# RWKV-7 recurrence with a squared-ReLU feed-forward: a tile of their own for the small inverse blocks, an earlier transpose, and two weight transfers that change queues

## The chip, the cores and the metric

The kernel runs on one core of a Trainium2 chip. The metric is device time in microseconds, from launch to the end of the last instruction; the time of a kernel is the median of its runs. The profile is that of one execution.

The engines go by these names: PE is the matmul engine (PEld its loading of weights), DVE the vector engine, ACT the scalar engine, POOL the GpSimd engine, SP the engine that here only issues transfers. [...]

## The reference

The first half is a recurrence over 768 tokens for 4 batches of 8 heads with 40 channels each. The second is a feed-forward layer on the 3072 token rows of 320 channels.

```python
B, H, S, D = 4, 8, 768, 40
state = zeros((B, H, D, D))
for t in range(S):
    y[:, :, t] = einsum('bhd,bhde->bhe', rt, state)
    Sa = einsum('bhde,bhe->bhd', state, at)
    state_decay = state * wt[:, :, None, :] - einsum('bhd,bhe->bhde', Sa, bt)
    state = state_decay + einsum('bhd,bhe->bhde', vt, kt)
# y (B, H, S, D) -> x (B*S, H*D) = (3072, 320)
h = maximum(x @ w_in, 0.0)          # w_in (320, 2048)
out = (h * h) @ w_out               # w_out (2048, 320)
```

The weights reach the kernel as 64-bit floats and are turned into 32-bit ones on the chip.

## The kernel before

The kernel cuts the 768 tokens into chunks of 128, so that there are 6 chunks of each of 4 batches, 24 in all. The step from token to token inside a chunk becomes a triangular system per head. Its inverse is solved on POOL (`solve`) and goes through memory (`kept_t`) to the place where the matmuls read it (`inverses`). For the first six chunks (those with `u < FINE`) only the inverses of 32x32 blocks are solved, and PE joins two of them into one of 64x64. Chunk 0 is handled ahead of the main loop, chunks 1 to 5 within it.

These are the parts that the change touches. First, where the short-lived tiles of the joining lie: in slices of `hidden`, the big tile which later holds the hidden layer, or for chunk 5 in the two tiles `own_`.

```python
hidden = single("hid", [128, NF + 1, GB * C])           # NF = 16, GB * C = 256
free_words = hidden.rearrange("p f t -> p (f t)")
wide = [room[:, 4 * WI * i:4 * WI * (i + 1)] for i in range(2)] + [free_words[:, :4 * WI]]
lent = [free_words[:, 2 * DM * i:2 * DM * (i + 1)] for i in range(3)]
own_ = [single(f"raw{i}", [128, 2 * DM]) for i in range(2)]

def spare(name, i):
    n = ("mv", "turned", "blocks", "joins").index(name)
    t_ = hidden[:, NF - 2 * n - i % 2] if i <= B else own_[n // 2][:, n % 2 * H * Q:(n % 2 + 1) * H * Q]
    return t_.rearrange("p (h t) -> p h t", h=H)
```

`wide` and `lent` are the places into which the raw 64-bit weights are fetched: some in the space of the finished weights (`room`, a view of `w_out`), some in the low slices of `hidden`. The raw weights are unpacked piece by piece, some steps per turn of the main loop:

```python
def rounding():
    now = None
    for n in range(len(pieces) + 1):
        before, now = now, None
        if before:
            bits = before[-1]
            nc.scalar.activation(bits, bits, Act.Relu, bias=lowest, scale=float(1 << 23))            # L257
        if n < len(pieces):
            dst, raw = pieces[n]
            words = raw.rearrange("p (f e) -> p f e", e=2)
            nc.scalar.activation(dst, words[:, :, 0].bitcast(U32), Act.Copy, scale=2.0 ** -32)       # L261
        yield
        if before:
            d_, hi, mant, bits = before
            nc.vector.scalar_tensor_tensor(d_.bitcast(I32), hi, -(1 << 31), bits, ...)               # L265
            nc.vector.scalar_tensor_tensor(d_, mant, 2.0 ** -20, d_, Alu.mult, Alu.mult)             # L266
            finished[0] += 1
            for m_ in then.get(n - 1, ()):
                later(lambda m_=m_: fetch_weights(m_, nc.sync), 1)                                   # L248
        if n < len(pieces):
            hi = words[:, :, 1].bitcast(I32)
            # ... two tensor_scalar (L274, L275) and one tensor_tensor (L276) into PSUM ...
            now = dst, hi, mant, bits
        yield
```

Then the joining itself. `queue` is the sync queue.

```python
def inverses(i, g, queue=nc.sync):
    # ...
    if u >= FINE:
        # ... T is loaded from kept_t as it is (L449)
    else:
        blocks = spare("blocks", i)
        for col in range(classes(u)):
            queue.dma_start(out=blocks[col::classes(u)], in_=kept[col].rearrange(...))               # L455
    if "N" not in g:
        # ... loads N from kept_n (L458) and, for the first six chunks, g["joins"] from kept_m (L462)
    if u >= FINE:
        return
    yield
    upper_ = spare("turned", i)
    nc.vector.transpose(upper_.rearrange("p h t -> p (h t)"), blocks.rearrange("p h t -> p (h t)"))  # L467
    for n in range(2):
        nc.scalar.activation(T[:, :, n * Q:(n + 1) * Q], blocks, Act.Copy, scale=which[:, n:n + 1])  # L469
    # ... 16 products of joins and upper_ into p_ (the first small product), p_ to mv (L478)
    yield
    # ... 16 products of mv and blocks (the second small product), to T (L485)
    yield
```

`rest(i + 1)` prepares the next chunk while `chain(i)` runs the present one. The yields are its stages; the main loop takes one stage of each generator in turn, so that they set the order of instructions in each engine's queue.

```python
def rest(i, g):
    # ... stage 2: k transposed
    # stage 3: kvT, ends; joining = inverses(i, g) and, for the early chunks, its first stage (the loads)
    yield
    g["A"] = masked("A", 4, kT, aT)                       # L331
    yield
    # ... rT and vT: r and v transposed by PE, copied by ACT (L513, L515)
    yield
    if c > 0:
        # ... the state times its decay
    g["RV"] = masked("RV", 4, vT, rT)                     # L331
    yield
    # ... the decay transposed by PE (L530)
    yield
    # ... k and b times the inverse decay (L534); the state transposed (L540)
    yield
    yield from joining
    yield
```

`early(m)` works further ahead: it turns the decay of a later chunk and makes its system, with the scans L354 and L355, the reciprocals L358 and L359, bT (L362), aT (L363) and N (L370). `chain(i)` makes xr, minus_x, xnT, RX (L331) and the output tokens (L612). Ahead of the main loop the first weights are fetched beside the solves:

```python
solve(1, {8: lambda: weights_by(0, nc.gpsimd), 20: lambda: take(2, own)})
run(r0)
run(join)
weights_by(2, nc.sync)
solve(2, {4: lambda: weights_by(1, nc.gpsimd)})
```

Fetch 0 feeds pieces 0 and 1 of the unpacking, fetch 1 pieces 2 and 3 (both in the space of `w_out`), fetch 2 pieces 4 and 5 (in the low eight slices of `hidden`). Turn 0 of the main loop unpacks 4 pieces, turn 1 seven, turns 2 and 3 eight each. The first four turns carry no feed-forward matmuls; these begin with turn 4.

Of the kernel before, what the change touches and what calls it, by code (L numbers as in the profile page):

```python
# [17 lines left out]
def kernel(  # L18
# [22 lines left out]
    nc = tc.nc  # L41
    ctx.enter_context(tc.manual_schedule())
    B, H, S, D = r.shape
# [17 lines left out]
    for h, d, n in ((6, 0, D), (7, 0, D), (5, HALF, D - HALF)):  # L61
        while n:
# [5 lines left out]
            d, n = d + m_, n - m_  # L68
# [13 lines left out]
    def psum(pool):  # L82
        name = "ps_" + pool.name[-1]
        return pool.tile([128, 512], FP32, tag=name, name=name)
# [7 lines left out]
    def new(name, shape, bufs):  # L92
        return work.tile(shape, FP32, tag=name, name=name, bufs=bufs)
# [22 lines left out]
    class Ring:  # L116
# [6 lines left out]
        def next(self):  # L123
            self.at = (self.at + 1) % len(self.tiles)
            return self.tiles[self.at]
# [168 lines left out]
    Q = HC // 2  # L294
# [5 lines left out]
    FINE = 4  # L300
# [3 lines left out]
    unit_of = {first + n: u for u, (first, nb) in enumerate(units) for n in range(nb)}  # L304
# [13 lines left out]
    def products(l_, r_):  # L318

        ps = [quads(psum(ps_w)) for _ in range(2)]  # L320
        for q in range(NP):
            for e in range(2):
                rows = slice(e * DP, e * DP + D)
                mm(ps[e][:, q], l_[rows, q, :], r_[rows, q, :], True)
        return ps

    def masked(name, bufs, l_, r_):
        res = []
        for p_ in products(l_, r_):
            t_ = new(name, [128, NP, 128], bufs)  # L330
            nc.vector.tensor_tensor(t_, p_, over4(upper), Alu.mult)  # L331
            res.append(t_)
        return res

    turned = lambda nm, bufs: new(nm, [128, NP, 128], bufs)
# [1 line left out]


    def spare(name, i):
        n = ("mv", "turned", "blocks", "joins").index(name)  # L340
        t_ = hidden[:, NF - 2 * n - i % 2] if i <= B else own_[n // 2][:, n % 2 * H * Q:(n % 2 + 1) * H * Q]
        return t_.rearrange("p (h t) -> p h t", h=H)

# [68 lines left out]
    def solve(u, between={}):  # L412

        first, nb = units[u]
        fine = u < FINE
        size = Q if fine else HC
        cols = classes(u)
        rows = 128 // cols
        part = part_of(u)
        words = size // cols * size  # L420
        at = u * Q * Q // 2 if fine else 0
        ts = solved[:, at:at + words]
        nc.gpsimd.memset(ts, 0.0)
        for col in range(cols):
            nc.gpsimd.memset(ts[col * rows:(col + 1) * rows, col::size + cols], -1.0)
        t3 = ts.rearrange("p (j t) -> p j t", t=size)
        for s in range(size - 1):
            if s in between:
                between[s]()
            n, m_ = s // cols + 1, size - 1 - s  # L430
            at = s * size + s + 1 if s < Q else Q * HC + (s - Q) * (Q + 1) + 1
            p_ = new("half_p", [128, 528], 1)[:, :n * m_].rearrange("p (j t) -> p j t", j=n)
            nc.gpsimd.tensor_tensor(p_, part[:, at:at + m_].unsqueeze(1).to_broadcast([128, n, m_]),  # L433
                                    t3[:, :n, s:s + 1].to_broadcast([128, n, m_]), Alu.mult)
            nc.gpsimd.tensor_tensor(t3[:, :n, s + 1:], t3[:, :n, s + 1:], p_, Alu.subtract)  # L435
        to = kept_t[u]
        to = to.rearrange("n b h f k j t -> (n b h f k) (j t)") if fine else to.rearrange("n b h f j t -> (n b h f) (j t)")
        nc.gpsimd.dma_start(out=to, in_=ts)
# [3 lines left out]
    def inverses(i, g, queue=nc.sync):  # L442
        bb, c = order[i]
        u = unit_of[i]
        kept = kept_t[u][:, i - units[u][0]]
        g["T"] = T = new("T", [128, H, HC], 2)
        if u >= FINE:
            for col in range(classes(u)):
                queue.dma_start(out=T[col::classes(u)], in_=kept[col].rearrange("h f j t -> (f j) h t"))  # L449
        else:  # L450


            blocks = spare("blocks", i)
            for col in range(classes(u)):
                queue.dma_start(out=blocks[col::classes(u)], in_=kept[col].rearrange("h f k j t -> (f k j) h t"))  # L455
        if "N" not in g:
            g["N"] = new("N21", [HC, H, HC], 2)
            queue.dma_start(out=g["N"], in_=kept_n[i])  # L458
            if u < FINE:
                g["joins"] = spare("joins", i)  # L460
                for half in range(2):
                    queue.dma_start(out=g["joins"][half * HC:half * HC + Q], in_=kept_m[i][half])  # L462
# [4 lines that stand above are left out]
        nc.vector.transpose(upper_.rearrange("p h t -> p (h t)"), blocks.rearrange("p h t -> p (h t)"))  # L467
        for n in range(2):
            nc.scalar.activation(T[:, :, n * Q:(n + 1) * Q], blocks, Act.Copy, scale=which[:, n:n + 1])  # L469
        small = lambda: psum(ps_w)[:, :H * Q].rearrange("p (h t) -> p h t", h=H)  # L470
        p_ = small()
        mv = spare("mv", i)
        ends_ = [(slice(half * HC, half * HC + Q), slice(half * HC + Q, (half + 1) * HC)) for half in range(2)]
        for one, two in ends_:
            for h in range(H):
                mm(p_[two, h], g["joins"][one, h], upper_[one, h], True)
        for one, two in ends_:
            nc.scalar.copy(mv[two], p_[two])  # L478
        yield
        p_ = small()  # L480
        for one, two in ends_:
            for h in range(H):
                mm(p_[one, h], mv[two, h], blocks[two, h], True)
        for one, two in ends_:
            nc.scalar.copy(T[one, :, Q:], p_[one])  # L485
        yield
# [4 lines left out]
    def rest(i, g):  # L491
        bb, c = order[i]
        x_ = loaded.pop(i)
        dec = g["dec"]
        up, down, aT = dec[:, UP], dec[:, DOWN], dec[:, A_, :, :C]
        ends = new("ends", [128, NP], 2)
        g["up"], g["aT"] = up, aT
        yield

        kT, rT = turned("kvT", 1), turned("rT", 2)  # L500
        kT_ = turn(x_["k"])
        yield
        nc.vector.tensor_tensor(kT, kT_, down[:, :, 1:C + 1], Alu.mult)
        nc.vector.tensor_copy(ends, down[:, :, 0])
        joining = inverses(i, g) if i else iter(())
        if soon(i):
            next(joining, None)
# [3 lines that stand above are left out]
        while "v" not in x_:  # L511
            line.pop(0)[1]()
        nc.scalar.copy(rT, turn(x_["r"]))  # L513
        vT = turned("kvT", 1)
        nc.scalar.copy(vT, turn(x_["v"]))  # L515
        g["rT"] = rT
        yield
        if c > 0:
            st = states.tiles[bb]
            f_ = new("f", [128, NP, 2], 1)  # L520
            nc.vector.tensor_tensor(f_[:, :, 0], ended[bb], ends, Alu.mult)
            nc.vector.tensor_copy(f_[:, :, 1], f_[:, :, 0])
            nc.vector.tensor_tensor(f_, f_, same, Alu.mult)
            nc.vector.tensor_tensor(st[:, :, :, :D], st[:, :, :, :D],
                                    f_.unsqueeze(3).to_broadcast([128, NP, 2, D]), Alu.mult)
        g["RV"] = masked("RV", 4, vT, rT)
        yield
        p_ = psum(ps_w)
        for q in range(NP):
            nc.tensor.transpose(p_[:, q * 128:(q + 1) * 128], down[:, q, 1:C + 1], ident)  # L530
        inv = p_.rearrange("t (h d) -> t h d", h=H)[:, :, :D]
        yield
        for nm in ("k", "b"):
            nc.vector.tensor_tensor(x_[nm][:, :, :D], inv, x_[nm][:, :, :D], Alu.mult)  # L534
            g[nm] = x_[nm]
        g["v"] = x_["v"]
        if c > 0:
            p_ = psum(ps_c)
            for q in range(NP):
                nc.tensor.transpose(p_[:, q * 128:(q + 1) * 128], st[:, q].rearrange("p e d -> p (e d)"), ident)  # L540
            sd = g["sd"] = new("sd", [128, NP, 2, DP], 2)
            nc.scalar.copy(sd.rearrange("p q e d -> p q (e d)"), quads(p_))
# [3 lines that stand above are left out]
# [159 lines left out]
    def weights_by(n, queue):  # L705
        if weights:
            fetch_weights(n, queue)
# [37 lines left out]
    solve(1, {8: lambda: weights_by(0, nc.gpsimd), 20: lambda: take(2, own)})  # L745
    run(r0)
    run(join)
    weights_by(2, nc.sync)
    solve(2, {4: lambda: weights_by(1, nc.gpsimd)})
    for gen in (e0, e1, e2, e3):  # L750
        run(gen)
    flush()
# [10 lines left out]
    for i in range(len(order)):  # L763
        bb, c = order[i]
        n, before = share.get(i, (TOTAL, 0))
# [56 lines left out]
```

## Time and profile before

| what | value |
|---|---|
| time, median of 3 runs | 1173.26 us (1169.07 to 1174.62) |
| span of the profiled execution | 1171.8 us |
| PE busy | 1041.4 us, 89% of the span |
| POOL busy | 650.8 us, 56% |
| DVE busy | 482.4 us, 41% |
| ACT busy | 245.6 us, 21% |
| moved by DMA | 113.48 MB in 262366 packets, 244164 of them under 512 B |

A line of the page's second part cuts the span into 40 equal slices of 29.3 us; each digit is the busy share of one slice in tenths, and in the line PEclk the share of its full clock that PE was granted. In a timeline, a line gives start and duration, the engine, the source line, the operation and "output<-inputs". A bracket at the end tells how long the engine sat idle before it and what it then had to wait for. SPq is the queue of the sync engine, so its lines are transfers being issued. A line such as L87 or L331 belongs to a helper which many parts of the kernel call; the tile names tell which part it is.

### The profile page before, as it was taken

The numbers are of one execution on the slowest core, as the hardware profiler recorded it, in microseconds if no ns is written. First come the engines' busy times: TensorE is split into PE (matmuls) and PEld (weight loads), VectorE is DVE, ScalarE is ACT, GpSimd is POOL, SyncE is SP. The second block draws the span as 40 slices with busy tenths as digits, with TensorE's granted clock in tenths as the row PEclk, the third lists the DMA queues.
The fourth block names the chain that finished last, engine by engine and source line by source line (L and its number), as shares of the span: only waits on it lengthen the run. The fifth ranks groups of instructions, "written<-read, shape, count | busy, mean of one in ns | idle before, by whom it ended". The sixth has DMA issues, their size and how long they took to land.

```text
span 1171.8 us, 19330 instructions
## 1 busy us (share of the span) xinstructions
PE 1041.4 (89%) x7632; PEld 822.7 (70%) x7632; DVE 482.4 (41%) x1004; ACT 245.6 (21%) x547; POOL 650.8 (56%) x1128
## 2 busy tenths in 40 slices
PE   6496475768999999899899999999999999999998
PEld 5385464655877777777677777777777787777666
DVE  5467474672636515515515514524423243230211
ACT  2123121222222211212211212112122122121211
POOL 5885715882884499950499950599958840000000
PEclk9755555557999998999999999998999999999999
DMA  9989828347454850561861561831444224140000
GB/s 115 158 146 212 164 82 149 116 89 166 77 117 104 163 117 34 105 152 39 155 130 46 96 137 57 169 81 52 95 113 84 56 57 89 24 83 12 6 12 12
DMA packets 262366, 113.48 MB, mean 97 GB/s; under 512 B 244164, under 2 KB 250436, under 8 KB 260612
## 3 DMA queue, kind: packets, MB, share of 16 engines
q1 hardware_dynamic: 257956, 93.24, 39.1%
q0 software_dynamic: 3232, 18.88, 6.6%
q8 instruction: 60, 0.98, 0.4%
q10 hardware_dynamic: 1088, 0.13, 0.1%
q14 instruction: 30, 0.25, 0.1%
HBM read 75.77 MB, written 34.48 MB: 94 GB/s over the span
## 4 chain that ended last, share of the span: by engine, by line
PE 68%; DVE 10%; DMA 9%; SPq 4%; issue 4%; POOL 3%; ACT 2%; DVEq 0%; POOLq 0%; ACTq 0%
PE ps_f L87 32%; PE ps_c L87 19%; PE ps_w L87 11%; DMA in_v<-in_v_dram 4%; PE ps_w L315 4%; SPq L108 2%; DVE decay L358 1%; DMA w_out<-in_moe_w_in_dram 1%; DVE decay L359 1%; PE ps_w L530 1%; POOL half_t L435 1%; POOL half_p L433 1%; PE ps_c L540 1%; SPq L142 1%; SPq L248 1%
## 5 line engine op out<-in xcount | busy, mean ns | idle before, releaser
L433 POOL TENSOR_TENSOR half_p<-half_n,half_t 128x70 f32<-128x70 f32 (+52 forms) x502 | 289.1, 576 | 107.3 <-DMA half_n<-kept_d 57.8
L435 POOL TENSOR_TENSOR half_t<-half_t,half_p 128x70 f32<-128x70 f32 (+52 forms) x502 | 314.3, 626 | 39.3
L640 DVE TENSOR_TENSOR hid<-ps_f,hid 128x256 f32<-128x256 f32 x176 | 73.9, 420 | 343.2 <-ACT hid L639 342.9
L87 PE MATMUL ps_f<-w_out,hid 128*128 128x320 f32 x704 | 207.7, 443 | 0.1
L87 PE MATMUL ps_f<-tokens,w_in 128*128 128x256 f32 x704 | 196.7, 406 | 0.0
L87 PEld LDWEIGHTS ps_f<-w_out,hid 128*128 128x128 f32 x704 | 130.2, 193 | 49.3 <-issue 2.0
L87 PEld LDWEIGHTS ps_f<-tokens,w_in 128*128 128x128 f32 x704 | 123.1, 193 | 42.4 <-issue 29.7
L639 ACT ACTIVATE hid<-ps_f 128x256 f32<-128x256 f32 x176 | 67.4, 383 | 264.3 <-PE ps_f L87 263.9
L87 PE MATMUL ps_f<-tokens,w_third 64*128 64x256 f32 x352 | 85.7, 419 | 6.7 <-DVE hid L640 5.1
L410 POOL DMA_DIRECT2D half_n<-kept_d x18 | 8.9, 502 | 138.5 <-DMA kept_d<-N 138.4
L87 PEld LDWEIGHTS ps_c<-xr,T 64*64 64x64 f32 x768 | 54.4, 149 | 22.0 <-issue 11.7
L87 PE MATMUL ps_c<-xr,T 64*64 64x40 f32 x768 | 60.1, 240 | 5.6 <-DMA T<-kept_t 2.7
L87 PEld LDWEIGHTS ps_f<-tokens,w_third 64*128 64x128 f32 x352 | 39.8, 187 | 33.9 <-DVE hid L640 23.0
L354 DVE TENSOR_TENSOR_SCAN decay<-ps_w,ones 128x64 f32<-128x64 f32 x88 | 23.5, 267 | 85.2 <-PE ps_w L315 77.7
L87 PEld LDWEIGHTS ps_c<-in_v,A 128*128 128x128 f32 x384 | 52.9, 215 | 2.3
L87 PE MATMUL ps_w<-rT,xnT 40*128 40x128 f32 x384 | 37.5, 317 | 16.7 <-DVE RV L331 16.1
L87 PE MATMUL ps_c<-in_v,A 128*128 128x40 f32 x384 | 51.9, 300 | 0.0
L87 PE MATMUL ps_w<-hid 32*32 32x32 f32 x320 | 17.1, 237 | 38.8 <-DVE hid L467 23.8
L87 PEld LDWEIGHTS ps_w<-rT,xnT 40*128 40x128 f32 x384 | 30.9, 214 | 27.0 <-DVE RV L331 22.8
L87 PEld LDWEIGHTS ps_w<-hid 32*32 32x32 f32 x320 | 15.9, 150 | 41.2 <-issue 40.6
L612 DVE TENSOR_TENSOR tokens<-ps_c,dec 128x512 f32<-128x512 f32 x24 | 16.5, 689 | 68.0 <-PE ps_c L87 68.0
L315 PE MATMUL ps_w<-ident,in_ab 128*128 128x128 f32 x192 | 32.1, 318 | 13.8 <-ACT rT L513 9.9
(144 smaller groups left out, 1466.2 us busy)
## 6 DMA issues: line engine op xcount, KB each, us to landing
kept_e<-decay SPq DMA_DIRECT2D x22, 780.0 KB
dec<-kept_e SPq DMA_DIRECT2D x22, 780.0 KB
half_n<-kept_d POOLq DMA_DIRECT2D x12, 384.0 KB, 9.9
half_n<-kept_d POOLq DMA_DIRECT2D x6, 768.0 KB, 11.2
in_w<-in_w_dram SPq DMA_DIRECT2D x24, 160.0 KB
in_ab<-in_b_dram SPq DMA_DIRECT2D x24, 160.0 KB
in_ab<-in_a_dram SPq DMA_DIRECT2D x24, 160.0 KB
in_k<-in_k_dram SPq DMA_DIRECT2D x24, 160.0 KB
```

The costliest lines, as they stand in the source:

```text
L87: nc.tensor.matmul(o, l_, r_, start=start, stop=True, skip_group_check=True)
L108: later(lambda: queue.dma_start(out=out_, in_=in_), steps)
L142: nc.sync.dma_start(out=t_[:, :, :D], in_=src[bb, :, c * C:(c + 1) * C, :].rearrange("h t d -> t h d"))
L248: queue.dma_start(out=to, in_=src.bitcast(I32))
L315: nc.tensor.transpose(p_[:, q * 128:(q + 1) * 128], pair(x_, q), ident)
L354: nc.vector.tensor_tensor_scan(up[:, q, MID + 1:C + 1], wT[:, q, MID:], ones, 1.0, Alu.mult, Alu.mult)
L358: nc.vector.reciprocal(down[:, :, MID + 1:C + 1], up[:, :, MID + 1:C + 1])
L433: nc.gpsimd.tensor_tensor(p_, part[:, at:at + m_].unsqueeze(1).to_broadcast([128, n, m_]), t3[:, :n, s:s + 1].to_broadcast([128, n, m_]), ...
L435: nc.gpsimd.tensor_tensor(t3[:, :n, s + 1:], t3[:, :n, s + 1:], p_, Alu.subtract)
L612: nc.vector.tensor_tensor(t_, y_, g["up"][:, :, :C], Alu.mult)
L639: nc.scalar.activation(h_, p_, Act.Relu)
L640: nc.vector.tensor_tensor(h_, p_, h_, Alu.mult)
```

## The change

The blocks get a tile of their own, one buffer of 128 partitions by 1 KB, instead of a slice of `hidden` (of `own_` for chunk 5). The tiles for the joins move up into the place that this leaves in `spare`. The transposing of the blocks, with their two scaled copies into T, becomes a stage by itself. For chunks 1 to 5 it is taken directly behind the masked product RV, two stages of `rest` sooner than before; the two small products stay where they were. For chunk 0 it stays in place too. Last, weight fetch 1 goes to the sync queue ahead of the third solve and fetch 2 to the GpSimd queue inside it; before it was the other way round.

Its purpose is that the transpose and the copies should be done before PE comes to the first small product, that the blocks no longer share a tile with other data, and that the fetch which is unpacked first is also fetched first.

```diff
-        n = ("mv", "turned", "blocks", "joins").index(name)
+        n = ("mv", "turned", "joins").index(name)
...
-            blocks = spare("blocks", i)
+            blocks = new("blocks", [128, H, Q], 1)
...
         for n in range(2):
             nc.scalar.activation(T[:, :, n * Q:(n + 1) * Q], blocks, Act.Copy, scale=which[:, n:n + 1])
+        yield
         small = lambda: psum(ps_w)[:, :H * Q].rearrange("p (h t) -> p h t", h=H)
...
         g["RV"] = masked("RV", 4, vT, rT)
+        if i and unit_of[i] < FINE:
+            next(joining)
         yield
...
-    weights_by(2, nc.sync)
-    solve(2, {4: lambda: weights_by(1, nc.gpsimd)})
+    weights_by(1, nc.sync)
+    solve(2, {4: lambda: weights_by(2, nc.gpsimd)})
```

## The prediction

> **What bounds the kernel now.** I read the page's slices first, because a share of busy time over the whole span hides that this kernel has two regimes.
>
> ```profile
> PE 1041.4 (89%) x7632; PEld 822.7 (70%) x7632; DVE 482.4 (41%) x1004; ACT 245.6 (21%) x547; POOL 650.8 (56%) x1128
> ...
> PE   6496475768999999899899999999999999999998
> ...
> PEclk9755555557999998999999999998999999999999
> DMA  9989828347454850561861561831444224140000
> ```
>
> One slice is 29.3 us. From the eleventh slice on (about 290 us) PE is busy nine tenths or more at nearly full clock: there the end is set by matmul work, which the change leaves as it is. In the first ten slices PE is half busy at half clock, so something else holds it. All gain or loss must come from there. Next I asked for busy time by stage. The stages are the first turns of the main loop; I took their ends from the timeline (turn 0 starts near 58 us, turn 4, the first that carries feed-forward matmuls, at about 275). Columns: stage, length, busy us of PE, PEld, DVE, ACT and POOL (instructions), granted clock, DMA share, GB/s.
>
> ```profile
> 58.00:107.00 49.00, 35.48 (x312) 32.60 (x310) 31.46 (x59) 13.95 (x27) 39.16 (x115) 0.60 0.85 168
> 107.00:168.00 61.00, 36.65 (x289) 32.94 (x288) 36.68 (x67) 13.53 (x26) 24.65 (x68) 0.50 0.63 138
> 168.00:225.00 57.00, 36.66 (x269) 31.97 (x269) 30.92 (x66) 13.39 (x32) 36.53 (x71) 0.53 0.61 128
> 225.00:275.00 50.00, 36.10 (x285) 31.91 (x284) 32.23 (x72) 15.16 (x35) 34.60 (x66) 0.57 0.46 111
> 275.00:330.00 55.00, 53.85 (x372) 40.45 (x372) 27.22 (x59) 11.94 (x28) 38.15 (x73) 0.95 0.59 105
> ```
>
> No engine fills turns 0 to 3; waits do. So I read the timeline of each turn for the long idle times. Columns: start, duration, engine, line, operation, output and inputs, and in brackets the idle time before it and what ended it.
>
> ```profile
> 90.38 0.69 DVE L274 TENSOR_SCALAR ps_f<-w_out 128x512 int32<-128x512 int32 x1 [3.50 <-DMA w_out<-in_moe_w_in_dram]
> ...
> 125.11 1.33 SPq L455 DMA_DIRECT2D hid<-kept_t  x2
> ...
> 133.23 0.69 DVE L265 SCALAR_TENSOR_TENSOR w_in<-hid,ps_f 128x512 int32<-128x512 int32 x1 [12.95 <-DMA hid<-kept_t]
> ...
> 137.28 1.12 PE L315 MATMUL ps_w<-ident,in_w 128*128 128x128 f32 x4 [14.41 <-DVE A L331]
> ...
> 158.25 0.68 DVE L363 TENSOR_TENSOR decay<-ps_w,decay 128x512 f32<-128x512 f32 x1
> ...
> 162.15 0.43 DVE L467 STREAM_TRANSPOSE hid<-hid 128x256 f32<-128x256 f32 x1
> 162.69 1.69 PE L87 MATMUL ps_w<-hid 32*32 32x32 f32 x32 [6.49 <-issue]
> ...
> 164.31 2.08 PE L87 MATMUL ps_w<-decay,bT 40*128 40x128 f32 x16
> ...
> 196.88 0.49 ACT L261 ACTIVATE w_out<-hid 128x320 f32<-128x320 uint32 x1 [16.05 <-DMA hid<-kept_t]
> 196.93 0.49 DVE L265 SCALAR_TENSOR_TENSOR w_out<-hid,ps_f 128x320 int32<-128x320 int32 x1 [15.18 <-DMA hid<-kept_t]
> ...
> 246.49 0.49 DVE L274 TENSOR_SCALAR ps_f<-hid 128x320 int32<-128x320 int32 x1 [6.36 <-DMA hid<-kept_m]
> ```
>
> This is the finding. L265, L261 and L274 unpack the feed-forward weights from the low slices of "hid". The transfer they wait for (L455) puts the small inverse blocks into another slice of the same tile, and they use none of it. The order of the built program says the same: in each of the three turns these instructions carry waits for the two block transfers (in turn 3 too, where the profile names kept_m, which lands last). In order behind them stands everything of DVE, and PE waits for DVE's A. So turns 1, 2 and 3 hold **false waits** of 12.95, 15.18 and 6.36 us.
>
> A second wait is smaller. PE's first small product (162.69) stands ahead of the product of decay and bT and needs the 32x32 transpose, L467. L467 stands last in DVE's row of a turn, so although L363 had freed bT at 158.9, that product began at 164.31.
>
> **What the Trainium skill says.** "Perfetto Trace Analysis", section "Optimization Strategy": a kernel can have regimes, and the gaps within a regime are what to explain. The trace agrees: PE's longest wait is 14.4 us ahead of 275 us and 1.7 us behind it. "DMA: Bandwidth & Descriptors", section "Issuing engines are not separate DMA queues": all queues share the same 16 DMA engines, and another queue only saves issue time. So changing queues is worth its place in time, not bandwidth. The trace has nothing against it: the fetch that GpSimd issued at 78.88 was first read at 90.37. "TensorE: Matmul & The Clock Gate", section "What's actually happening": idle windows put the matmul clock to half. The trace shows 0.50 in turn 1 and 1.00 from 290 to 400 us. Shorter gaps might raise it; I count nothing for that.
>
> **The change part by part.** No instruction with real work is added; the ten scaled copies, the transposes and the products remain. The blocks get a tile of 1 KB a partition, with one buffer. The joins move by two slices of hid. In the new order the three unpacking instructions carry no wait for the blocks, and L467 itself does, directly after RV. That is later in DVE's row than the old false wait and earlier than the old L467.
>
> Turn 0. Weight fetch 1 is needed before fetch 2 (it feeds pieces 2 and 3). It now goes out near 56.6 us on the sync queue instead of 78.88 on GpSimd, so the 3.50 us wait goes. L467 moves ahead and the small product fits into PE's idle time: bT's product followed L363 (end 98.2) only at 100.38, another 2.1. Sum 5.6; I count 5.
>
> Turn 1. Without the stall DVE goes on at 120.3. The work from 133.23 to the end of RV (147.5) took 14.3 us, so it reaches L467 at 134.6, when the blocks have landed (133.2). The 12.95 vanish nearly whole. The second wait gives 164.31 less 158.9 = 5.4. Sum 18.3; I count 17.
>
> Turn 2. The stall began at 181.75, but PE had in_r at 187.7 and in_v at 188.8; with the transpose (1.1), two copies (0.6 each), the product (2.1) and RV (1.3), DVE is at L467 at about 194.5 and waits there for the blocks until 196.9. Then 0.5 of transpose and 2.2 of unpacking: RX at 199.6 instead of 210.3, 10.7 us sooner. PE was free at 215.8 and began bT's product at 221.68: 5.9 more. Sum 16.6; I count 15.
>
> Turn 3. 6.36, and bT's product at 265.1 (end of the state's transposes) instead of 270.42: 5.3. Sum 11.7; I count 9, since the loads of r and v may bind first.
>
> Turn 4 on: PE is busy 53.85 of 55 us, so I count 0. Together 46, of 52 at most. From this I take 5 more for new waits on queues that get fuller: **41 us**, 1173 - 41 = 1132.
>
> **Rivals.** (a) The wait only moves: L467 stands in DVE's row and needs the same transfer, so a late landing stalls DVE there. For it: turn 2, where I find 2.4 us. Against it: some 14 us of DVE work lie between old and new place. If the landing slips by 5 us in turns 1 to 3, 15 us go: 1147. (b) The DMA engines become the bound. Share times length gives 41.7, 38.4, 34.8 and 23.0 us of DMA work in turns 0 to 3; in turns of about 44, 44, 42 and 41 us that is 95%, 87%, 83% and 56%. So turn 0 could give nothing and turn 1 half: about 1145. (c) Nothing comes of it, because a load (in_r, in_v, the weights unpacked just before) lands just behind the blocks. Against it: PE had in_r and in_v by 188.8, 8 us ahead of the blocks. That would give 1155 to 1173. (d) GpSimd's inverses become late. It finishes the solution for chunks 6 and 7 at 264.3, and they are read at 350.5: 86 us of slack, more than turns 0 to 4 can lose.
>
> **Range and chances.** The middle is my sum. (a) or (b) in part make the upper end, 1152. All 52 us and a few of clock or smoother queues make the lower end, 1114. Faster by over 2% means below 1149.8, which needs 24 of the 46 us: 0.88. Within 2%: 0.10, if a transfer binds in two turns. Slower by over 2% would need a new stall of 23 us, which I can't find: 0.02.
>
> **What would show it.** Right: no DVE or ACT unpacking line behind hid<-kept_t; the wait at L467 in turns 1 to 3 is 0 to 4 us each; PE's small product no longer follows an idle time of 4 us or more; turns 0 to 3 take some 175 us instead of 217; the stretch behind them keeps its length of some 895 us. Wrong: L467 or T's copies (L469) wait 10 us for blocks<-kept_t (rival a); a DMA share over 0.95 through turns 0 and 1 (b); an idle time of the old size ending on in_r, in_v or a weight fetch (c). If the stretch from turn 4 on changes by more than 5 us, my assumption that it stays is wrong.

## The result and the profile after

| | before | after |
|---|---|---|
| time, median of 4 runs each | 1171.18 us (1169.07 to 1174.62) | 1136.15 us (1134.51 to 1136.86) |
| ratio after / before | | 0.9696, 95% interval 0.9665 to 0.9727 |
| span of the profiled execution | 1171.8 us | 1135.1 us |

The change saves 35 us, 3.0%. The prediction said 1132 us and 41 us.

First the slices of the page of the changed kernel; one slice is now 28.4 us.

```profile
PE 1029.9 (91%) x7632; PEld 811.9 (72%) x7632; DVE 482.1 (42%) x1004; ACT 246.2 (22%) x547; POOL 651.7 (57%) x1129
...
PE   6385787799999999999999999999999999999998
```

PE is busy nine tenths from the ninth slice on, two slices sooner. Where turns 1 to 3 lie, the digits are 7, 8, 7, 7 (fifth to eighth slice); before they were 4, 7, 5, 7, 6, 8 (fifth to tenth). The busy times hardly moved; the waits did. Next, the busy time by stage. The columns are stage, length, busy us of PE, PEld, DVE, ACT and POOL (instructions), granted clock, DMA share and GB/s; the first four lines are turns 0 to 3, the last is all from turn 4 on.

```profile
58.00:102.40 44.40, 29.52 (x296) 26.83 (x294) 30.09 (x56) 11.93 (x24) 36.43 (x105) 0.65 0.85 158
102.40:149.20 46.80, 35.62 (x301) 32.38 (x301) 37.97 (x68) 15.70 (x31) 28.00 (x79) 0.61 0.87 187
149.20:190.30 41.10, 32.95 (x275) 28.97 (x273) 30.22 (x65) 13.34 (x31) 21.68 (x49) 0.59 0.84 192
190.30:231.80 41.50, 31.48 (x278) 27.77 (x277) 33.33 (x74) 15.66 (x36) 37.03 (x58) 0.66 0.56 124
231.80:1135.10 903.30, 870.67 (x6260) 670.28 (x6260) 322.11 (x682) 178.11 (x408) 488.94 (x699) 0.97 0.39 85
```

Turns 1 and 2 took 61 and 57 us in the kernel before; they take 47 and 41. The DMA engines carry much the same bytes there in less time, so their share rises from 0.63 and 0.61 to 0.87 and 0.84; in turn 0 it stays at 0.85. Then the timeline of the changed kernel, at the places that the prediction named.

```profile
77.78 2.62 SPq L455 DMA_DIRECT2D blocks<-kept_t  x4
...
88.88 0.91 ACT L469 ACTIVATE T<-blocks,which 128x256 f32<-128x256 f32 x2 [6.25 <-DMA blocks<-kept_t]
88.90 0.45 DVE L467 STREAM_TRANSPOSE hid<-blocks 128x256 f32<-128x256 f32 x1 [4.44 <-DMA blocks<-kept_t]
...
98.58 2.08 PE L87 MATMUL ps_w<-decay,bT 40*128 40x128 f32 x16 [8.02 <-DVE decay L363]
...
118.70 0.68 DVE L265 SCALAR_TENSOR_TENSOR w_in<-hid,ps_f 128x512 int32<-128x512 int32 x1
...
125.15 1.33 SPq L455 DMA_DIRECT2D blocks<-kept_t  x2
...
133.99 0.45 DVE L467 STREAM_TRANSPOSE hid<-blocks 128x256 f32<-128x256 f32 x1 [2.02 <-DMA blocks<-kept_t]
...
142.58 1.09 PE L87 MATMUL ps_w<-hid 32*32 32x32 f32 x32
...
178.70 0.45 DVE L467 STREAM_TRANSPOSE hid<-blocks 128x256 f32<-128x256 f32 x1 [2.11 <-DMA blocks<-kept_t]
...
218.40 0.43 DVE L467 STREAM_TRANSPOSE hid<-blocks 128x256 f32<-128x256 f32 x1
```

In turn 1, L265 reads "hid" at 118.70, ahead of the issue of the blocks' transfer at 125.15; before, it stood still for 12.95 us until that transfer had landed. The blocks are now waited for only where they are used, in L467: 4.44, 2.02 and 2.11 us in turns 0, 1 and 2, nothing in turn 3. The small product at 142.58 carries no wait.

For all comparisons below I use one marker: the copy N<-ps_w on ACT (L370), which ends each of the turns 0 to 3, and as the fifth mark the first feed-forward matmul. Turn 0 is given by its end, turns 1 to 3 by their lengths. "Stretch" is from the first feed-forward matmul to the end of the span. Each row is one profile, in us.

| kernel | turn 0 ends | turn 1 | turn 2 | turn 3 | feed-forward begins | stretch |
|---|---|---|---|---|---|---|
| before | 102.53 | 63.94 | 57.36 | 48.74 | 274.63 | 897.2 |
| after | 100.70 | 46.95 | 41.73 | 40.34 | 231.78 | 903.3 |
| after_again | 99.09 | 48.22 | 43.61 | 40.88 | 233.86 | 897.0 |
| e1_own_tile | 101.08 | 52.08 | 44.13 | 45.48 | 244.83 | 897.3 |
| e7_rows_in_a_run | 102.85 | 49.99 | 44.15 | 45.52 | 244.56 | 900.2 |
| e2_early | 100.75 | 58.65 | 52.17 | 44.59 | 258.22 | 898.8 |
| e3_queues | 98.65 | 65.72 | 55.89 | 49.27 | 271.58 | 902.5 |
| e4_tile_and_early | 101.24 | 45.82 | 44.44 | 41.37 | 234.93 | 899.4 |
| e5_one_stage_later | 98.00 | 48.13 | 40.59 | 39.13 | 227.91 | 902.3 |
| e5_again | 99.46 | 48.20 | 37.94 | 40.19 | 227.85 | 903.9 |
| e6_fetch2_step12 | 98.10 | 46.69 | 42.96 | 39.27 | 229.07 | 905.7 |
| e8_later_and_step12 | 97.03 | 47.12 | 39.37 | 39.05 | 224.63 | 898.8 |
| e9_from_chunk_2 | 98.66 | 45.83 | 45.05 | 41.28 | 232.88 | 903.4 |
| e10_later_old_queues | 100.55 | 45.46 | 41.34 | 40.85 | 230.26 | 903.4 |

Two rows of the same kernel differ by up to 1.6 us in the end of turn 0 and by up to 2.7 us in a later turn, so a smaller difference, in one profile, decides nothing by itself.

After against before: turns 0 to 3 gained 1.8, 17.0, 15.6 and 8.4 us, and the feed-forward began 42.85 us sooner. But the span fell by only 36.7 us; 6.1 us came back in the stretch behind. So two questions were open: why turn 0 gave so little, and what lengthened a stretch that the change doesn't touch.

### The profile page after: what moved, and what is told of

It reads as the page before. It is cut to its first block, busy times and chain, and to the rows that moved or that the text cites. A ratio compares the mean times of both kernels' runs of the same rounds, so it can differ in the third digit from the quotient of the medians.

```text
span 1135.1 us, 19336 instructions
## 1 busy us (share of the span) xinstructions
PE 1029.9 (91%) x7632; PEld 811.9 (72%) x7632; DVE 482.1 (42%) x1004; ACT 246.2 (22%) x547; POOL 651.7 (57%) x1129
## 4 chain that ended last, share of the span: by engine, by line
PE 69%; DVE 11%; DMA 10%; SPq 3%; POOL 2%; issue 2%; ACT 2%; DVEq 0%; POOLq 0%; ACTq 0%
PE ps_f L87 34%; PE ps_c L87 19%; PE ps_w L87 11%; PE ps_w L315 3%; DMA in_v<-in_v_dram 3%; DVE decay L358 1%; DVE decay L359 1%; PE ps_w L533 1%; SPq L108 1%; DMA in_r<-in_r_dram 1%; DMA blocks<-kept_t 1%; POOL half_t L435 1%; POOL half_p L433 1%; DMA in_w<-in_w_dram 1%; PE ps_c L543 1%
## 5 line engine op out<-in xcount | busy, mean ns | idle before, releaser
L87 PE MATMUL ps_f<-tokens,w_in 128*128 128x256 f32 x704 | 199.5, 410 | 0.0
L87 PEld LDWEIGHTS ps_c<-xr,T 64*64 64x64 f32 x768 | 54.9, 150 | 23.6 <-issue 13.8
L87 PE MATMUL ps_w<-rT,xnT 40*128 40x128 f32 x384 | 36.4, 309 | 12.6 <-DVE RV L331 12.1
L545 ACT COPY sd<-ps_c 128x512 f32<-128x512 f32 x20 | 11.7, 586 | 144.8 <-PE ps_c L543 144.8
L87 PE MATMUL ps_w<-decay,bT 40*128 40x128 f32 x352 | 28.4, 307 | 14.6 <-DVE decay L363 14.6
L370 ACT COPY N<-ps_w 128x512 f32<-128x512 f32 x48 | 25.8, 589 | 63.8 <-PE ps_w L87 44.2
```

The costliest lines, as they stand in the source:

```text
L87: nc.tensor.matmul(o, l_, r_, start=start, stop=True, skip_group_check=True)
L370: nc.scalar.copy(t_[:, e * NP:(e + 1) * NP], p_)
```

## The experiments

### The parts one by one

Each of the first four kernels starts from the kernel before. Their runs stand beside runs of the kernel before with a median of 1175.99 us.

**The own tile alone** (e1_own_tile).

```diff
-        n = ("mv", "turned", "blocks", "joins").index(name)
+        n = ("mv", "turned", "joins").index(name)
-            blocks = spare("blocks", i)
+            blocks = new("blocks", [128, H, Q], 1)
```

> The kernel before with the blocks in a tile of their own, and nothing else of the change. Theory 'false waits': the unpacking of the weights no longer waits for the blocks, so the waits of 12.95, 15.18 and 6.36 us in turns 1 to 3 go; the transpose stays last in its turn and PE goes on waiting for it. Turns 1, 2, 3 shorter by about 12, 12 and 6 us, turn 0 as before: about 30 us less, some 1141 us. Rival 'early transpose': the tile is only tidier and the wait for the same transfer moves to the transpose itself: under 8 us less, 1163 or more.

Measured: 1145.31 us (1143.75 to 1148.63), ratio 0.9761 (0.9724 to 0.9798). Turns 1 to 3 gained 11.9, 13.2 and 3.3 us. With no instruction and no transfer moved in time order, the tile alone brings the greater part of the gain. (The joins lie two slices further on; the next run leaves them where they were and gives the same time, so that isn't the cause.)

**Blocks still in "hid", but each transfer writes neighbouring partitions** (e7_rows_in_a_run). In the kernel before, each block transfer writes every n-th partition of the slice (every second or fourth one). This kernel leaves that row order out: the same bytes land in the same slice as consecutive rows, so the joining works on rows in the wrong places, and its output is not the reference's. It asks only what the waits do.

```diff
-  queue.dma_start(out=blocks[col::classes(u)], in_=...)
+  queue.dma_start(out=blocks[col * 128 // classes(u):(col + 1) * 128 // classes(u)], in_=...)
```

> The kernel before, blocks still in the big tile, but each block transfer writes a run of neighbouring partitions instead of every second (or fourth) one. The rows then lie in another order, so this kernel leaves the right order of rows out; its work is the same. Theory 'false waits by stride': what makes the unpacking wait isn't the shared tile as such, but that the range of a transfer with a stride over the partitions is taken to cover other slices; the waits go as in the run with an own tile, and the time is the same as there within 3 us, about 1141 us. Rival 'shared tile': as the tile is still shared, the waits of 12.95, 15.18 and 6.36 us stay, about 1171 us.

Measured: 1146.52 us (1144.33 to 1152.76), ratio 0.9776 (0.9732 to 0.982): within 1.2 us of the own tile. The timeline of this kernel shows the unpacking of turn 1 and the transfer behind it:

```profile
120.43 0.68 DVE L265 SCALAR_TENSOR_TENSOR w_in<-hid,ps_f 128x512 int32<-128x512 int32 x1
...
126.06 1.34 SPq L455 DMA_DIRECT2D hid<-kept_t  x2
```

L265 carries no wait, although the blocks still lie in "hid". So sharing a tile is not by itself the cause; here it took a destination with a step over partitions as well. In the trace of the kernel before, L265 at 133.23 waits on two semaphores more than L265 here. The likely reading is that the program's dependencies take a stepped destination as a range that also covers the other slices; the range itself I could not see.

**The earlier transpose alone** (e2_early).

```diff
             nc.scalar.activation(T[:, :, n * Q:(n + 1) * Q], blocks, ...)
+        yield
...
         g["RV"] = masked("RV", 4, vT, rT)
+        if i and unit_of[i] < FINE:
+            next(joining)
         yield
```

> The kernel before with only the transpose two stages sooner; the blocks stay in the big tile. Theory 'false waits': the three long waits stay where they are and only PE's wait for the transpose goes: 2 us in turn 0, 5.4, 5.9 and 5.3 us in turns 1 to 3, some 16 us less, 1155 us. Rival 'early transpose': this is the main part of the change, 30 us or more less, 1141 us or below.

Measured: 1157.99 us (1156.85 to 1161.34), ratio 0.987 (0.9833 to 0.9907). Turns 0 to 3 gained 1.8, 5.3, 5.2 and 4.2 us, near the 2.1, 5.4, 5.9 and 5.3 that the second wait counted. The false waits stay (the third, in turn 3, is 6.99 us); the timeline of this kernel has the first two:

```profile
131.47 0.69 DVE L265 SCALAR_TENSOR_TENSOR w_in<-hid,ps_f 128x512 int32<-128x512 int32 x1 [13.28 <-DMA hid<-kept_t]
...
191.15 0.49 DVE L265 SCALAR_TENSOR_TENSOR w_out<-hid,ps_f 128x320 int32<-128x320 int32 x1 [16.39 <-DMA hid<-kept_t]
```

**The exchange of the two weight transfers alone** (e3_queues).

```diff
-    weights_by(2, nc.sync)
-    solve(2, {4: lambda: weights_by(1, nc.gpsimd)})
+    weights_by(1, nc.sync)
+    solve(2, {4: lambda: weights_by(2, nc.gpsimd)})
```

> The kernel before with only the two weight transfers exchanged. Theory: DVE's wait of 3.50 us for the second fetch in turn 0 goes, and nothing else: 2 to 4 us less, 1168 us. Rival: the exchange only moves the load on the same DMA engines, the other fetch then delays the blocks: within 1 us of before.

Measured: 1173.88 us (1167.45 to 1176.63, 12 runs), ratio 0.9978 (0.9952 to 1.0004): no change that can be told from none. In its profile turn 0 ends 3.9 us sooner, close to the 3.50 us of the wait that it removes, but turns 1 to 3 together give back 0.8, and its stretch is 5.3 us longer.

### Why turn 0 gave so little

**The whole change without the exchange** (e4_tile_and_early: after, with the last two lines of the diff undone).

> The whole change without the exchange of the two weight transfers. Alone the exchange took 4 us from turn 0 (its end came at 98.65 instead of 102.53 us), but alone the early transpose ends turn 0 at 100.75 and the whole change at 100.70. Theory (in turn 0 the early transpose waits for the blocks, and this wait sets the turn's end, so the exchange finds nothing left to save): within 2 us of the whole change, some 1136, and turn 0 ends at 100.7. Rival (the exchange still gives its 2 to 4 us): some 1139, turn 0 ends after 102.

Measured: 1135.84 us (1134.96 to 1136.21), ratio 0.967 (0.965 to 0.969); turn 0 ends at 101.24, 0.5 and 2.2 us later than in the two profiles of the changed kernel, and L467 waits 5.77 us for the blocks there. Beside the early transpose the exchange brings nothing that shows in the time.

**The transpose one stage later** (e5_one_stage_later): after, with `next(joining)` behind the transposes of the decay instead of behind RV.

```diff
         g["RV"] = masked("RV", 4, vT, rT)
-        if i and unit_of[i] < FINE:
-            next(joining)
         yield
         p_ = psum(ps_w)
         ... the transposes of the decay ...
+        if i and unit_of[i] < FINE:
+            next(joining)
```

> The whole change, with the early transpose one stage later (behind the transposes of the decay instead of directly behind RV). Theory (the transposes of the whole change wait 4.44, 2.02 and 2.11 us for their blocks in turns 0 to 2, and DVE and PE are held up by that): these waits shrink below 1 us; turn 0 ends 3 us sooner, turns 1 and 2 take 1 to 2 us less each; about 1130. Rival (what ends last in these turns is another wait, the one for the decay or for the weights): turn ends move by less than 1 us, about 1136. Second rival: the later transpose brings back the wait of the small product, and the time goes up by 5 us or more, as without the earlier transpose.

Measured: 1130.52 us (1128.57 to 1132.52), ratio 0.9626 (0.9601 to 0.9651). The transposes of turns 0, 1 and 2 in the timeline of this kernel:

```profile
88.38 0.43 DVE L467 STREAM_TRANSPOSE hid<-blocks 128x256 f32<-128x256 f32 x1
...
137.43 0.43 DVE L467 STREAM_TRANSPOSE hid<-blocks 128x256 f32<-128x256 f32 x1
...
180.07 0.43 DVE L467 STREAM_TRANSPOSE hid<-blocks 128x256 f32<-128x256 f32 x1
```

All three waits of L467 are gone. (ACT's copies still wait 3.07 and 2.36 us for the blocks in turns 0 and 2.) The feed-forward begins at 227.91, 3.9 to 6.0 us sooner than in the two profiles of the changed kernel. The gain lies in turn 0 and turns 2 and 3; turn 1 gained nothing, which was not expected.

**Weight fetch 2 issued later in the third solve** (e6_fetch2_step12).

```diff
-    solve(2, {4: lambda: weights_by(2, nc.gpsimd)})
+    solve(2, {12: lambda: weights_by(2, nc.gpsimd)})
```

> The whole change, with weight fetch 2 issued later in the third solve (at its twelfth step instead of its fourth). Theory (in turn 0 fetch 2, which starts 1.2 us after the blocks' transfer, competes with it for the DMA engines): without it the blocks land 2 to 4 us sooner than 88.9 us and turn 0 ends by as much sooner; about 1133. Rival (the landing of the blocks is set by the transfer itself, many small packets): they land at 88 to 89 as before and the time stays within 1.5 us, or goes up if fetch 2 is then read before it has landed.

Measured: 1134.52 us (1130.66 to 1136.5), ratio 0.9649 (0.962 to 0.9678). The time is as expected, but also within the scatter of the changed kernel; the trace decides. Its timeline:

```profile
78.75 2.62 SPq L455 DMA_DIRECT2D blocks<-kept_t  x4
...
83.05 0.91 ACT L469 ACTIVATE T<-blocks,which 128x256 f32<-128x256 f32 x2 [0.93 <-DMA blocks<-kept_t]
83.86 0.43 DVE L467 STREAM_TRANSPOSE hid<-blocks 128x256 f32<-128x256 f32 x1
...
86.46 2.56 POOL L248 DMA_DIRECT2D hid<-in_moe_w_in_dram  x5
```

Fetch 2 in the timeline of the changed kernel:

```profile
78.95 2.56 POOL L248 DMA_DIRECT2D hid<-in_moe_w_in_dram  x5
```

From the start of the issue, the blocks need 4.3 us (78.75 to 83.05). In the changed kernel, where fetch 2 goes out 1.2 us behind them, at 78.95, they need 11.1 us (77.78 to 88.88). In after_again and the two profiles of e5, with fetch 2 in its early place, they need 9.6, 8.0 and 10.8 us by the same reading; in e4, where fetch 1 has that place, L467 gets them after 11.3 us; and in e8 below, the second run with a late fetch, ACT reads them 5.1 us behind the start of the issue without any wait. So the weight fetch in that place held the blocks up by 3 to 7 us, though it was issued later and through another engine's queue. This agrees with the Trainium skill, "DMA: Bandwidth & Descriptors", section "Issuing engines are not separate DMA queues": all queues end on the same 16 engines and interleave there.

**The later transpose with the transfers on their old queues** (e10_later_old_queues: e5, with the exchange undone), and **e5 again** beside it (e5_again).

> The whole change with the transpose one stage later, but with the two weight transfers on their old queues. With the early transpose the exchange was worth nothing (1135.84 without it, 1136 to 1138 with it), while alone it took 3.9 us from turn 0. Theory (the early transpose's wait for the blocks hid it): with this wait gone the exchange is worth 2 to 4 us again, so turn 0 ends at 100 to 102 here and the time is some 1133. Rival (the blocks and not the weights bind turn 0 in any order): turn 0 ends at 98 to 99 and the time is 1130.

> The whole change with the transpose one stage later, once more, to stand beside the others on the same chip. Its first time was 1130.52 us (1128.57 to 1132.52), its turn 0 ended at 98.0 and its feed-forward began at 227.9. Expected: within 2 us of that time, turn 0 within 0.7 us; in the stretch behind the start of the feed-forward half-clock time between 30 and 48 us, and a length of 880.3 us plus half of it.

Measured: 1129.87 us (1123.41 to 1135.89, 6 runs), ratio 0.9623 (0.959 to 0.9657), and for e5_again 1133.95 us (1129.35 to 1138.11), ratio 0.9651 (0.9621 to 0.968). The times don't tell the two apart; that of e10 is the one which the rival expected. e5_again missed what was expected of it: its time is 3.4 us above its first one instead of within 2, and its turn 0 ends 1.5 us later instead of within 0.7. The timeline of e10 does show the old wait for fetch 1, and PE behind it:

```profile
90.06 0.69 DVE L274 TENSOR_SCALAR ps_f<-w_out 128x512 int32<-128x512 int32 x1 [3.42 <-DMA w_out<-in_moe_w_in_dram]
...
92.64 1.62 PE L87 MATMUL ps_w<-hid 32*32 32x32 f32 x32 [5.30 <-DVE hid L467]
```

Turn 0 ends at 100.55, against 98.00 and 99.46 with the exchange. That is where the theory expected it, 1.1 to 2.6 us later, but two profiles of one kernel differ by up to 1.6 us. So the exchange takes a wait out of turn 0 once the transpose no longer stands there; what that is worth, these times don't show. The second profile of e5 also shows how far the landing of the blocks moves from run to run: ACT had them at 85.59 in the first and at 89.83 in the second.

**The early transpose from chunk 2 on only** (e9_from_chunk_2: after, with chunk 1 left as before).

```diff
-        if i and unit_of[i] < FINE:
+        if i > 1 and unit_of[i] < FINE:
             next(joining)
...
+        if i == 1:
+            next(joining)
         yield from joining
```

> The whole change, with the early transpose only from chunk 2 on; for chunk 1, which turn 0 prepares, the transpose stays directly ahead of the small product as in the kernel before. Theory (in turn 0 the early place costs what the exchange of the transfers brings): turn 0 ends at 98.0 to 98.7, as with the exchange alone (98.65), 1.5 to 2.5 us sooner than in the whole change; turns 1 to 3 as in the whole change, so some 1134. Rival (the blocks are late in turn 0 wherever they are read): turn 0 ends after 99.5, some 1136.

Measured: 1135.89 us (1132.84 to 1138.38), ratio 0.967 (0.9645 to 0.9695). Turn 0 ends at 98.66, as with the exchange alone (98.65). But turn 2 takes 45.05 us, with L467 waiting 3.45 us for the blocks instead of 2.11, where the theory expected turns 1 to 3 as in the whole change. The feed-forward begins at 232.88, between the two profiles of the changed kernel, and the whole is no better than that kernel. Whether turn 2 always takes back what turn 0 gains, one profile can't say.

**Both helpful edits together** (e8_later_and_step12: the edits of e5 and e6).

> The two helpful edits together: the transpose one stage later, and weight fetch 2 at the twelfth step of the solve. Alone each brought the end of turn 0 from some 100 to 98 us. Theory (both take away the same wait for the blocks in turn 0, so together they give little more than one): turn 0 ends between 96.5 and 98, the feed-forward begins at 225 to 228 us, and the time is within 3 us of the later transpose alone, 1127 to 1131. Rival (they add up): the feed-forward begins near 223, some 1126. Behind its start the stretch should be 880.3 us plus half of the half-clock time, within 1 us.

Measured: 1124.37 us (1121.28 to 1136.24, 6 runs), ratio 0.9589 (0.9552 to 0.9626). It beats both kernels: its interval lies wholly below that of the change (0.9665 to 0.9727). Turn 0 ends at 97.03, 1.0 to 2.4 us sooner than with e5, and the feed-forward begins 3.2 us sooner; that is between the two theories, while the time is below both (1127 to 1131 and 1126). The remaining distance to e5_again, some 6 of 9.6 us, is not explained by the turns; the stretch was 5.1 us shorter in e8's profile, which leads to the other question.

### What lengthened the stretch behind turn 4

**The changed kernel once more** (after_again).

> The changed kernel itself once more. In its first profile the stretch from turn 4 on took 903.3 us where the kernel before took 897.2, and in it PE's clock was at half for 53.9 us instead of 41.0. Theory A (where the clock falls to half is a matter of chance from run to run, and the stretch grows by half of such time): the stretch differs from 903.3 by some us, up or down, and again equals about 876.5 us plus half of the half-clock time. Theory B (the change itself has brought new waits there, which recur): 903.3 within 1 us, with half clock at the same places.

Measured: 1138.12 us (1132.59 to 1140.02), ratio 0.9683 (0.965 to 0.9715). In its profile the stretch is 897.0 us, 6.3 us shorter than in the first profile of the same kernel. (The half-clock times in the expectation are counted from a wrong zero. From the start of the span they are 46.8 us for after and 33.3 for before, and the constant is 880.3 instead of 876.5.) Half-clock time in the second profile is 33.1 us.

So the 6.1 us of the first pair of profiles need no new wait in the changed kernel: the same kernel differs by as much from run to run. PE's idle time in the stretch hardly differs either: 31.4 us before, 32.6 and 31.8 us in the two profiles after. Over 14 profiles, of all kernels of this case, I added up the time at half clock in the stretch and took half of it from the stretch's length: 11 of the 14 results lie within 0.9 us of 880.3. The other three are e6 (881.8), e5_again (878.6) and e9 (877.8), whose cause I don't know. A microsecond at half clock costs about half a microsecond there, and nearly all of the scatter of the stretch, 897.0 to 905.7, is this. (In e5_again the half-clock time was 50.5 us, a little over the range expected.)

What starts such a time can be seen in the windows of the trace. In these lines PE's busy time is the first number behind the length and the clock is the third from the end. First the changed kernel:

```profile
848.61:852.03 3.42, 1.68 (x14) 1.25 (x14) 0.42 (x1) 0.80 (x2) 2.95 (x7) 1.00 0.62 149
852.03:855.44 3.41, 3.41 (x20) 2.50 (x19) 0.00 (x0) 0.42 (x1) 3.02 (x6) 0.50 1.06 297
855.44:858.85 3.41, 3.41 (x21) 2.59 (x20) 0.42 (x1) 0.80 (x2) 3.02 (x6) 0.50 1.47 151
858.85:862.27 3.42, 3.42 (x12) 2.19 (x10) 0.42 (x1) 0.38 (x1) 3.11 (x5) 0.50 0.41 72
```

And the kernel before at the same place of its program:

```profile
888.22:891.63 3.41, 3.15 (x24) 2.70 (x23) 0.42 (x1) 0.67 (x3) 3.02 (x6) 1.00 0.30 74
891.63:895.05 3.42, 2.53 (x24) 1.98 (x24) 0.42 (x1) 0.58 (x2) 2.96 (x6) 1.00 1.02 256
895.05:898.46 3.41, 3.41 (x29) 2.59 (x28) 0.85 (x2) 1.19 (x3) 3.02 (x5) 1.00 1.30 215
```

At this point PE waits for its inverses. The timelines have the wait, again first in the changed kernel:

```profile
851.69 1.61 PE L87 MATMUL ps_c<-xr,T 64*64 64x40 f32 x16 [1.74 <-DMA T<-kept_t]
```

and then in the kernel before:

```profile
892.52 1.09 PE L87 MATMUL ps_c<-xr,T 64*64 64x40 f32 x16 [1.15 <-DMA T<-kept_t]
```

In the changed kernel the 1.74 us fall into one window, of which PE is busy 1.68 us of 3.42, and the three windows behind it run at half clock. In the kernel before the 1.15 us lie across the border of two windows, PE is busy 2.53 us of the worse one, and the clock stays full.

These two waits differ in length too. But all 14 profiles have this wait, of 1.08 to 2.02 us, and in e9 it is as short as in the kernel before and lies inside one window:

```profile
854.30 1.09 PE L87 MATMUL ps_c<-xr,T 64*64 64x40 f32 x16 [1.16 <-DMA T<-kept_t]
```

The windows of e9 there:

```profile
852.75:856.16 3.41, 2.25 (x23) 1.51 (x22) 0.42 (x1) 0.80 (x3) 2.95 (x6) 1.00 0.96 207
856.16:859.57 3.41, 3.41 (x20) 2.59 (x19) 0.42 (x1) 0.39 (x1) 3.02 (x6) 0.50 1.23 266
```

So the same length halves the clock in e9 and not in the kernel before. In 13 profiles the wait lies inside one window, of which PE is then busy 41 to 68%, and half clock follows in all 13; the kernel before is the only one in which it lies across a border.

## Why the prediction was right, and where it was off

**The false waits: right.** The time lies within the range, and the mechanism is the one named. No unpacking instruction waits for the blocks any more, and the own tile alone gave 11.9, 13.2 and 3.3 us in turns 1 to 3, where the steps counted 12.95, 10.7 and 6.36.

**The second wait: right in kind.** Early transposing alone gave 5.3, 5.2 and 4.2 us there. On top of the own tile (after less e1) it gave 5.1, 2.4 and 5.1, where the steps counted 5.4, 5.9 and 5.3; with after_again in place of after, 3.9, 0.5 and 4.6. The small second term is that of turn 2, where L467 now waits 2.11 us for its blocks; the prediction had found 2.4 us of wait there and put it on the side of the false waits. The sums agree: 17.0, 15.6 and 8.4 us against 17, 15 and 9. In the second profile of the changed kernel they are 15.7, 13.8 and 7.9.

**Turn 3: the amount right, the reason not.** The false wait was worth only half of its 6.36 us, so 8.4 us and not 11.7 came of both. The prediction had cut that sum to 9 because loads of r and v might bind; PE's longest wait for one of these in turns 0 to 3 of the changed kernel is 0.7 us. What happened is that PE had not stood still for all of DVE's 6.36 us. In turn 3 of the kernel before it waited 2.11 us for A and 5.50 us for RV; with the own tile (e1) the first wait is gone and the second is 4.31 us. That is 3.3 us, the gain of that turn. So the cut came out by luck.

**Turn 0: the failed step.** "Turn 0 ... Sum 5.6; I count 5": measured 1.8 and 3.4 us in the two profiles. The step let the weight wait of 3.50 us go, which it did, and put the earlier L467 in its place for nothing. It asked in turns 1 and 2 when the blocks land, but not in turn 0. They landed at 88.88, and L467 stood there from 84.5: rival (a), in the one turn without a false wait. Four runs show this from both sides. The exchange alone saves 3.9 us; beside the early transpose it saves nothing (e4). With the transpose one stage later the wait goes (e5), and with fetch 2 out of the way the blocks come 5.8 us sooner (e6, at 83.05). With both (e8) turn 0 gains 5.5 us, what the step had summed.

**The rivals.** Rival (a) held for 4.44 us in turn 0, and for 2.02 and 2.11 us in turns 1 and 2, inside the 0 to 4 us that the text allowed for turns 1 to 3. For rival (b) the prediction worked out DMA shares of 95, 87, 83 and 56% for turns 0 to 3; measured were 85, 87, 84 and 56%. In no turn did the mean share reach the 0.95 that was to show this rival. Yet in turn 0 it was contention that set the landing of the blocks, at a share of 0.81 from 76 to 90 us by the windows of the changed kernel: a mean share below 1 doesn't say that a small transfer lands in time. Rival (c) didn't come: apart from the blocks, PE's longest wait for a load in turns 0 to 3 is 1.2 us and DVE's 0.5 us. ACT has one of 7.8 us for raw weights in turn 2, but DVE didn't stand idle behind it. Nor did rival (d): in the stretch of the changed kernel PE's waits that end on T<-kept_t come to 2.4 us, in the kernel before to 2.7.

**The sum.** The discount from 46 to 41 us, for new waits, was right for the turns: the feed-forward began 42.85 us sooner in one profile of the changed kernel and 40.8 in the other. In the first, turn 0's 1.8 us instead of 5 make up all of the difference to 46.

**Turn 4 on: "I count 0", too simple.** The stretch grew by 6.1 us in the first profile of the changed kernel, which the prediction had named as the mark of a wrong assumption; in the second it shrank by 0.2 us. No new wait does this: PE's idle time there grew by 1.3 us in the first and by 0.5 in the second. The half-clock time differs from run to run, and about half of it is lost. The prediction had considered the clock only as a possible gain.

What stays open: the medians fell by 35.0 us in the first series (1171.18 to 1136.15) and by 36.4 in the second (1174.52 to 1138.12), not by 41. The second profile is of the fastest of its four runs, 5.5 us below their median, so its short stretch isn't typical; and the first series has a low median before, where later series have 1174.52 to 1175.99. Whether the average half-clock time is greater in the changed kernel these profiles can't say. The three kernels that keep the false waits (before, e2, e3) have stretches of 897.2 to 902.5, mean 899.5; the eleven profiles without them 897.0 to 905.7, mean 901.3; the ranges overlap.

## What to carry to other kernels

When an instruction waits for a transfer, check that it reads what the transfer wrote. If it doesn't, a tile of its own for the transfer's target, or, where the order of rows allows it, a target of neighbouring partitions, takes the wait away without touching any work; here that was some 30 of 35 us. When a consumer moves forward, look for the landing of its input in every turn in which it moves, also in those where nothing was wrong, and ask which large transfer is issued beside it. A small transfer that is soon needed should not share its moment with a large one that is not.

## What the runs showed of the hardware

- The granted clock changes in steps of 3.413 us, the lengths in the clock record being multiples of that. Of 89 such windows at full clock with PE busy less than 62%, 77 were followed by half clock; of 29 with 62 to 70%, 12; of 133 with 70 to 85%, 7; of 3015 with more, none (14 profiles, 245 windows in a row of each, from some 22 us behind the start of the feed-forward). The Trainium skill, "TensorE: Matmul & The Clock Gate", section "What's actually happening", gives this window of 3413 ns as free-running and says that the clock halves after at least one idle window of that length. The trace agrees on the window, but no idle window is needed: at the wait for the inverses, one in which PE rested for 1.08 to 2.02 us was enough in 13 profiles. So the same wait may cost its own length, or several us more, by how it falls on the grid: 1.15 us across a border cost no half clock in the kernel before, and 1.16 us inside one window were followed by two windows of it in e9.
- A weight transfer issued 0.7 to 1.6 us after the blocks' transfer, on a different queue, held the first one up: it took 8.0 to 11.1 us (after, after_again and the two profiles of e5) instead of 4.3 (e6).
